# An attention and MoE chain: row maxima on ScalarE's DMA queue, later inversion of the sums, a reordered prelude and other first banks

## The chip, the core and the metric

The kernel runs on one core of one Trainium2 chip. The metric is device time in microseconds (us), lower is better; a run is compared with other runs on the same chip. Five engines work side by side, each through its own queue in program order: TensorE (PE in the profile), VectorE (DVE), ScalarE (ACT), GpSimd (POOL) and SyncE (SP), which here does nothing but issue DMAs. An engine that meets a wait holds everything behind it in its own queue.

## The reference

Clustered attention (2 batches, 8 heads, 768 tokens, head size 64, 16 centroids per head), and then two MLPs on its output ("MoE" in the code).

```python
q_assign = np.argmax(np.einsum('bhsd,hcd->bhsc', q_n, c_n), axis=-1)   # q_n, k_n, c_n: normalised
k_assign = np.argmax(np.einsum('bhsd,hcd->bhsc', k_n, c_n), axis=-1)
mask = q_assign[:, :, :, None] == k_assign[:, :, None, :]
scores = np.where(mask, scale * np.matmul(q, k.transpose(0, 1, 3, 2)), -1000000000.0)
scores = scores - np.max(scores, axis=-1, keepdims=True)
attn = np.exp(scores)
attn = attn / (np.sum(attn, axis=-1, keepdims=True) + 1e-09)
x = np.matmul(attn, v)                       # reshaped to 1536 tokens x 512
x = np.maximum(x @ w_in, 0.0) ** 2 @ w_out   # first MLP, 512 -> 2048 -> 512
h = x @ w_in2                                # second MLP
return (h * np.cos(h)) @ w_out2
```

## The kernel before

Attention works on 8 pairs `n` of heads (one batch, two heads side by side on the 128 partitions). A pair has two halves `hf` of 384 query rows, and a half is 6 units of one 128-key tile each, so a pair has 12 units and the whole has 96. One loop over steps `g` from -9 to 95 does everything: step `g` computes `scores(g)` (four pairs of matmuls, L410, then the exponential on ScalarE, L414) and, nine units ahead, `s_max(g + 9)` (four matmuls, L359, and VectorE's maximum, L362); `pv` (L433) follows two units at a time in odd steps. PSUM is three double banks `unit`, handed out in turn by `unit()` and `give()`, and two banks `o_ps` for `pv`. An engine's queue has the order of the code; within a step the phases PRE, then scores, s_max and pv, then PROD, then POST are run, and the tables `prep`, `prep_second`, `prep_all` and `finish` say at which step and in which phase each piece stands.

The **row maximum** of a half reaches the scores through rows of the tile that the fourth pair of matmuls reads (`d["lq"]`, tile `set`). `max_parts` (L371, L372) joins the maxima, `max_rows` (L381) turns them on TensorE, and one step later `stage_max` copies them out of PSUM on ScalarE (`mr`, L388) and places them with two DMAs issued by SP (L391). This stands two steps ahead of the half's first scores.

The **sums** of a half: GpSimd adds up the exponentials (`add_up`, L426; VectorE does it for the last pair), `sums` turns them into column sums on TensorE (L448), `move_sums` copies (L456), `invert` takes the reciprocal on VectorE (L471), writes it to DRAM by SP (`row`, L473) and, once that has landed, reads it back spread over partitions with two more DMAs of SP (`rb`, L476). `divide` (L480) multiplies `o_ps` by it, `combine` (L492, L493) splits the result into two parts `xh` and `xl`. The next half that uses the same `o_ps` must wait for `divide`.

`invert` of one half and `stage_max` of a later one stand in neighbouring steps: `invert` in POST of a step `g` with `g % 6 == 3`, `stage_max` in PRE of the step after it. In SP's queue the order there is `row`, `rb`, `rb`, `mr`, `mr`.

Preparing a pair: loads of q and k, transposes (L249), a full copy and a high part on ScalarE (L265, L258), a low part on VectorE (L271), similarities with the centroids (`sims`, L300), their maximum (`by_token`, `at_max`), a one-hot code (`one_hot`), and the DMAs that place these (`stage`, `stage_own`, `stage_oh`). Pair 0 is prepared in the prelude ahead of the loop, pair 1 by `prep_second`. `warm` sends small matmuls whose result is not used.

Weights of the MLPs are split into a high and a low part by six instructions of VectorE and one copy of ScalarE (`w_split`, L152 to L161); one piece at a time is put at the end of steps 1, 4 and 7 of each pair in the middle of the loop (two pieces each), and in every step from step 75 on.

The MoE steps then run matmuls into `h_bank` (L604) and, two steps later, `y_mm` (L657) into four banks `y_banks` (both halves of `unit1` and `unit2`). The first step also does the last two `pv`, and `sums_here` of the last half into `unit2`.

Of the kernel before, what the change touches and what calls it, by code (L numbers as in the profile page):

```python
# [34 lines left out]
def tile_kernel(ctx: ExitStack, tc: tile.TileContext, q, k, v, centroids, w1i, w1o, w2i, w2o, out):  # L35
# [42 lines left out]


    firstf = perm.tile([P, P], F32, name="firstf")  # L80
    nc.gpsimd.memset(firstf, -1.0)
    nc.gpsimd.affine_select(
        firstf, firstf, pattern=[[1, P]], compare_op=ALU.is_gt, fill=0.0, base=0, channel_multiplier=-1
    )
    nc.gpsimd.affine_select(
        firstf.rearrange("p (b c) -> p b c", c=NC), firstf.rearrange("p (b c) -> p b c", c=NC),
        pattern=[[-NC, P // NC], [0, NC]], compare_op=ALU.is_ge, fill=0.0, base=0, channel_multiplier=1,
    )
    nc.gpsimd.tensor_tensor(firstf, firstf, ident, ALU.add)
    first_of = perm.tile([P, P], BF16, name="first_of")  # L90
    nc.vector.tensor_copy(first_of[:, : 2 * GC], firstf[:, : 2 * GC])
    nc.vector.tensor_scalar(first_of[:, 2 * GC :], firstf[:, 2 * GC :], -1.0, None, ALU.mult)
    oh_above = perm.tile([P, 1], F32, name="oh_above")
    nc.gpsimd.memset(oh_above[: 2 * GC], 0.5)
    nc.gpsimd.memset(oh_above[2 * GC :], -0.5)
    oh_scale = perm.tile([P, 1], F32, name="oh_scale")
    nc.gpsimd.memset(oh_scale[: 2 * GC], 1.0)
    nc.gpsimd.memset(oh_scale[2 * GC :], -BIG)
# [285 lines left out]
    def stage_max(n, hf):  # L384
# [5 lines left out]
        for j in range(2):  # L390
            nc.sync.dma_start(  # L391
# [116 lines left out]
    nc.scalar.activation(eps, half_t, AF.Exp)  # L508
    nc.gpsimd.memset(eps, 1e-9)
    nc.gpsimd.memset(cb, 0.0)  # L510

    def constants(e, i):
        inner = slice(R, P - R)
# [9 lines left out]
    constants(nc.vector, 0)  # L523
    warm(WARM)
    transpose_in(0, "q")
    transpose_in(0, "k")
    full_copy(0, "q")
    full_copy(0, "k")
    load_raw(1, "qk")
    nc.vector.tensor_tensor(c2, cw, cw, ALU.mult)  # L530
# [413 lines left out]
```

## Time and profile before

| what | us |
|---|---|
| runs (three) | 840.76, 838.58, 840.36 |
| median | 840.36 |
| the profiled execution | 838.24 |
| its span, first to last instruction | 836.5 |
| TensorE busy | 794.2 (95%) |
| VectorE busy | 592.6 (71%) |
| ScalarE busy | 357.2 (43%) |
| GpSimd busy | 177.3 (21%) |

The prelude takes the first 35 us or so, the attention loop lasts until about 292 us, and the MoE steps fill the rest. A busy TensorE is not one at its peak, and it is busy with warming matmuls too. The span is 1.7 us shorter than the execution's own time. What follows is read from the waits by engine, the timeline and the windows (busy time and granted clock of a stretch).

### The profile page before, as it was taken

The page shows a single profiled execution, that of the slowest core. Times are in us where ns is not written, and L with a number is a line of the kernel's source. Part 1 is how long each engine was busy: PE and PEld are TensorE (multiplying, and loading weights), DVE is VectorE, ACT ScalarE, POOL GpSimd, SP SyncE. Part 2 cuts the span into 40 slices and gives each one's busy share as a digit, 9 for nine tenths or more (in the row PEclk, how much of TensorE's full clock was granted, in tenths as well). Part 3 has the DMA queues.
Part 4 walks back from the last instruction along what each step waited for, and adds up shares of the span by engine and source line. Part 5 has one row for each costly group of instructions (what it writes and reads, how often), then busy time and mean ns, then how long its engine had stood idle before and what let it go on. Part 6 is the DMA issues. An engine that isn't in the chain of part 4 may idle for free.

```text
span 836.5 us, 11709 instructions
## 1 busy us (share of the span) xinstructions
PE 794.2 (95%) x4453; PEld 591.7 (71%) x4453; DVE 592.6 (71%) x944; ACT 357.2 (43%) x591; POOL 177.3 (21%) x203
## 2 busy tenths in 40 slices
PE   6999999899989799999999999999999999999997
PEld 4655555565555468888888888887788888888886
DVE  5766677676666899795977421969999866666665
ACT  2355454464444444444444342544343433333332
POOL 5254466456545033000000000001222100000000
PEclk9999999999999899999999999999999999999999
DMA  4525244333252390103740000653000100010001
GB/s 110 131 63 136 64 120 98 88 88 82 62 158 67 118 348 1 52 1 123 229 146 5 1 1 26 209 168 101 0 1 1 51 1 1 1 39 13 1 0 51
DMA packets 72376, 61.79 MB, mean 74 GB/s; under 512 B 41288, under 2 KB 63616, under 8 KB 72320
## 3 DMA queue, kind: packets, MB, share of 16 engines
q1 hardware_dynamic: 70768, 60.65, 24.7%
q8 instruction: 35, 0.57, 0.3%
q10 hardware_dynamic: 1552, 0.39, 0.2%
q14 instruction: 21, 0.17, 0.1%
HBM read 47.87 MB, written 5.29 MB: 64 GB/s over the span
## 4 chain that ended last, share of the span: by engine, by line
PE 77%; DVE 7%; DMA 6%; SPq 3%; ACT 2%; issue 2%; DVEq 0%; ACTq 0%
PE unit L657 29%; PE unit L604 16%; PE o_ps L604 14%; PE unit L410 7%; PE o_ps L433 5%; DMA set<-mr 4%; PE unit L359 3%; DMA row<-r 2%; DVE r L471 2%; SPq L476 1%; PE unit L448 1%; DVE ews L626 1%; PE unit L249 1%; DVE ews L625 1%; SPq L345 1%
## 5 line engine op out<-in xcount | busy, mean ns | idle before, releaser
L657 PE MATMUL unit<-w,ewr 128*128 128x512 f32 x576 | 140.2, 392 | 1.9 <-ACT ewr L638 0.7
L657 PE MATMUL unit<-ewr,w 128*128 128x512 f32 x576 | 141.9, 394 | 0.0
L362 DVE TENSOR_REDUCE m<-unit 128x2 f32<-128x768 f32 x96 | 91.4, 952 | 64.1 <-PE unit L359 63.6
L604 PE MATMUL unit<-xh,w 128*128 128x512 f32 x400 | 132.5, 392 | 3.4 <-ACT ews L619 1.9
L657 PEld LDWEIGHTS unit<-w,ewr 128*128 128x128 f32 x576 | 107.9, 188 | 26.8 <-ACT ewr L638 1.1
L657 PEld LDWEIGHTS unit<-ewr,w 128*128 128x128 f32 x576 | 107.9, 187 | 25.7
L604 PE MATMUL o_ps<-xh,w 128*128 128x512 f32 x368 | 121.2, 390 | 0.0
L414 ACT ACTIVATE p<-unit 128x768 f32<-128x768 f32 x96 | 77.7, 812 | 99.6 <-PE unit L410 97.7
L410 PE MATMUL unit<-set,set 64*128 64x384 f32 x512 | 87.4, 377 | 19.7 <-DMA set<-mr 17.3
L642 POOL TENSOR_TENSOR ewr<-ews,ewr 128x512 fp32r<-128x512 f32 x24 | 33.3, 1388 | 329.3 <-ACT ewr L638 297.6
L604 PEld LDWEIGHTS unit<-xh,w 128*128 128x128 f32 x400 | 75.1, 188 | 22.3 <-ACT ews L619 3.0
L642 DVE TENSOR_TENSOR ewr<-ews,ewr 128x512 fp32r<-128x512 f32 x72 | 49.5, 688 | 53.6 <-ACT ewr L621 51.4
L426 POOL TENSOR_TENSOR acc<-acc,p 128x384 f32<-128x384 f32 x84 | 86.7, 1067 | 3.2 <-ACT p L414 3.2
L410 PEld LDWEIGHTS unit<-set,set 64*128 64x128 f32 x512 | 48.0, 187 | 53.6 <-DMA set<-mr 22.5
L604 PEld LDWEIGHTS o_ps<-xh,w 128*128 128x128 f32 x368 | 69.1, 188 | 15.2
L629 ACT ACTIVATE ews<-ews,hpi 128x512 f32<-128x512 f32 x48 | 34.8, 725 | 103.0 <-DVE ews L628 103.0
L604 PE MATMUL unit<-xl,w 128*128 128x512 f32 x200 | 78.3, 391 | 0.0
L433 PE MATMUL o_ps<-p,rawv 128*64 128x384 f32 x384 | 74.6, 510 | 0.0
L604 PE MATMUL o_ps<-xl,w 128*128 128x512 f32 x184 | 71.9, 391 | 0.0
L153 DVE SCALAR_TENSOR_TENSOR w<-aux,aux 128x512 fp32r<-128x512 f32 x64 | 49.2, 768 | 1.8
L158 DVE SCALAR_TENSOR_TENSOR aux<-wraw,aux 128x512 f32<-128x512 uint32 x64 | 46.3, 723 | 1.8
L433 PEld LDWEIGHTS o_ps<-p,rawv 128*64 128x64 f32 x384 | 23.8, 139 | 30.6 <-issue 30.5
(128 smaller groups left out, 1080.8 us busy)
## 6 DMA issues: line engine op xcount, KB each, us to landing
wraw<-in_moe_w_in_dram SPq DMA_DIRECT2D x32, 512.0 KB, 4.2
wraw<-in_moe_w_out_dram SPq DMA_DIRECT2D x32, 512.0 KB, 3.9
rawq<-in_q_dram SPq DMA_DIRECT2D x8, 384.0 KB, 4.3
ext<-set SPq DMA_DIRECT2D x32, 96.0 KB, 2.1
rawv<-in_v_dram SPq DMA_DIRECT2D x8, 384.0 KB, 4.0
out_dram<-outs SPq DMA_DIRECT2D x12, 256.0 KB, 2.7
rawk<-in_k_dram SPq DMA_DIRECT2D x7, 384.0 KB, 5.0
rb<-row SPq DMA_DIRECT2D x28, 96.0 KB, 2.7
```

The costliest lines, as they stand in the source:

```text
L153: ve.scalar_tensor_tensor(w[:, 1], restf, 2.0**-20, power.bitcast(F32), ALU.mult, ALU.mult)
L158: cost(690, lambda: ve.scalar_tensor_tensor(restf, low, 2.0**-32, rest, ALU.mult, ALU.add)),
L359: nc.tensor.matmul(u[:, j, :HALF], lhsT=a[r, qs], rhs=b[r, ks], start=(p == 0), stop=(p == 1))
L362: nc.vector.tensor_reduce(d["m"][:, i, :, kh], u[:, :, :HALF], AX, ALU.max)
L410: nc.tensor.matmul(u[:, j, :HALF], lhsT=a[r], rhs=b[r, qs], start=(p == 0), stop=(p == len(ops) - 1))
L414: nc.scalar.activation(t, u[:, :, :HALF], AF.Exp, scale=SCALE)
L426: e.tensor_tensor(accs[hb][:, j], a[:, j], ptiles[u_][:, j], ALU.add)
L433: nc.tensor.matmul(o_ps[hf][j * D : (j + 1) * D, :HALF], lhsT=raw[n, "v"][:, kt, j, :], rhs=t[:, j], start=(kt == 0), stop=(kt == NT - 1),)
L604: nc.tensor.matmul(ph, lhsT=w[:, a, :], rhs=x[blk][:, a, :], start=(a == i == 0), stop=(a == KD - 1 and i == 2))
L629: nc.scalar.activation(e2, e2, AF.Sin, bias=hpi)
L642: e.tensor_tensor(al, e2, ah.bitcast(F32), ALU.subtract)
L657: nc.tensor.matmul(y, lhsT=a, rhs=b, start=(idx in opens and i == 0), stop=(idx in closes and i == 2))
```

## The change

Seven things change.

1. The two DMAs of `stage_max` are issued by ScalarE and no longer by SP. Of pair 0's one-hot DMAs the two for k are ScalarE's too.
2. `invert`, `divide` and `combine` stand one step later (10 and 15 for 9 and 14).
3. `max_rows` runs in a new phase LAST, behind the other PROD pieces of its step.
4. In the prelude the centroids are loaded first, and their chain (norm, reciprocal, transpose, `cb`) stands ahead of the transposes of q and k; constants move from VectorE to GpSimd, the making of `first_of` and its kin goes behind the first of these and its two copies to ScalarE.
5. The 24 warming matmuls between `sims(0)` and `one_hot(0)` go, and pair 1's transposes move in among them.
6. Pair 1's similarity steps move into steps -4 to -1, its stages to other steps.
7. The first MoE step's h goes to `banks[0]`, the second's to `y_banks[3]`, and from the third on the four banks rotate; `sums_here` of the last half uses `unit1`.

```diff
-    def stage_oh(n):
+    def stage_oh(n, e=nc.sync):
...
-                nc.sync.dma_start(
+                (e if i else nc.sync).dma_start(
...
         for j in range(2):
-            nc.sync.dma_start(
+            nc.scalar.dma_start(
                 d["lq"][OUTER[j], hf * HALF : (hf + 1) * HALF].bitcast(F32), mr[j * R : (j + 1) * R].bitcast(F32)
             )
...
+    nc.sync.dma_start(cw, centroids.rearrange("h c d -> (h c) d"))
     load_raw(0, "q")
     load_raw(0, "k", nc.scalar)
-    nc.sync.dma_start(cw, centroids.rearrange("h c d -> (h c) d"))
...
     stage(0, "k")
     stage_own(0)
+    sims(0)
+    by_token(0)
     low_part(0, "q")
     stage(0, "q")
-    low_part(0, "k")
-    sims(0)
-    warm(WARM_STEP)
-    by_token(0)
-    warm(WARM_STEP)
+    transpose_in(1, "q")
     at_max(0)
-    warm(WARM_STEP)
-    one_hot(0)
-    stage_oh(0)
-    transpose_in(1, "q")
     full_copy(1, "q")
     high_part(1, "q")
+    one_hot(0)
+    stage_oh(0, nc.scalar)
+    low_part(0, "k")
...
     load_raw(0, "v")
-    sims(1)
...
-    def h_bank(idx):
-        return banks[idx % (2 if idx < 4 else 4)]
...
-        ph = h_bank(idx)
+        ph = banks[(idx - 2) % 4] if idx > 1 else (banks[0], y_banks[3])[idx]
...
     prep_second = [
-        (-12, PROD, by_token),
-        (-12, POST, stage_own),
-        (-10, PROD, at_max),
-        (-8, PROD, one_hot),
-        (-11, POST, stage, "k"),
-        (-11, POST, stage, "q"),
-        (-7, PRE, stage_oh),
+        (-10, POST, stage_own),
+        (-8, POST, stage, "k"),
+        (-7, POST, stage, "q"),
+        (-7, PROD, sims),
+        (-6, PROD, by_token),
+        (-5, PROD, at_max),
+        (-4, PROD, one_hot),
+        (-4, POST, stage_oh),
         (1, PRE, load_raw, "v"),
     ]
     prep_all = [
         (6, PRE, max_parts, 0),
-        (6, PROD, max_rows, 0),
+        (6, LAST, max_rows, 0),
         (7, PRE, stage_max, 0),
         (12, PRE, max_parts, 1),
-        (12, PROD, max_rows, 1),
+        (12, LAST, max_rows, 1),
         (13, PRE, stage_max, 1),
     ]
 
     finish = [
         (8, PROD, sums),
         (9, PRE, move_sums),
-        (9, POST, invert),
-        (14, PRE, divide),
-        (14, POST, combine),
+        (10, POST, invert),
+        (15, PRE, divide),
+        (15, POST, combine),
     ]
...
         run(g, PROD)
+        run(g, LAST)
         run(g, POST)
...
-        0: [lambda: pv(NU - 2), lambda: pv(NU - 1), lambda: sums_here(last + 1, units[2])],
+        0: [lambda: pv(NU - 2), lambda: pv(NU - 1), lambda: sums_here(last + 1, units[1])],
```

ScalarE's queue ahead of a first half (pair 2, steps 9 to 11): `p` are the exponentials, `mxb` is `by_token`'s copy, `xh` `combine`'s, `mr` the row maxima. Before:

```order
L414 ACTIVATE p_1041<-unit_66 128x768
L318 COPY mxb_1060<-mx_1058 128x384
L388 CAST mr_1073<-unit_67 64x384
L414 ACTIVATE p_1085<-unit_65 128x768
L414 ACTIVATE p_1107<-unit_65 128x768
```

Now, in ScalarE's queue at the same place:

```order
L393 ACTIVATE p_1013<-unit_66 128x768
L297 COPY mxb_1029<-mx_1027 128x384
L471 CAST xh_87<-x_1001 128x128
L471 CAST xh_88<-x_1001 128x256
L367 CAST mr_1043<-unit_66 64x384
L370 DMA set_2_112<-mr_1043 32x384 x2
L393 ACTIVATE p_1055<-unit_67 128x768
L393 ACTIVATE p_1083<-unit_67 128x768
```

Two copies and two DMAs have come between `mxb` and the next exponential. In both listings the last two exponentials read the same unit, so the later one's scores wait for the earlier one's exponential.

VectorE's queue ahead of a second half (pair 2, steps 3 to 6): `r` is the reciprocal of the sums, `m` the maxima of `s_max`, `aux` and `w` are pieces of a weight split, the last row is the low part of q. Before:

```order
L471 RECIPROCAL r_1206<-r_1206 128x192
L362 TENSOR_REDUCE m_1222<-unit_67 128x2
L161 TENSOR_SCALAR aux_309<-top_312 128x512
L153 SCALAR_TENSOR_TENSOR w_1_0_1271<-aux_310,aux_309 128x512
L362 TENSOR_REDUCE m_1222<-unit_67 128x2
L271 TENSOR_TENSOR set_2_122<-unit_65,set_0_120 128x768
```

Now, in VectorE's queue at the same place:

```order
L341 TENSOR_REDUCE m_1196<-unit_66 128x2 x2
L450 RECIPROCAL r_1180<-r_1180 128x192
L140 TENSOR_SCALAR aux_279<-top_282 128x512
L132 SCALAR_TENSOR_TENSOR w_1_0_1247<-aux_280,aux_279 128x512
L341 TENSOR_REDUCE m_1196<-unit_66 128x2
L250 TENSOR_TENSOR set_2_108<-unit_67,set_0_106 128x768
```

The reciprocal has moved behind the maximum of the next step, right ahead of the two split pieces, the next maximum and the low part.

SP's queue around pair 1's first half, before:

```order
L473 DMA row_713<-r_678 4x192
L476 DMA rb_715<-row_713 64x384 x2
L391 DMA set_2_122<-mr_720 32x384 x2
L290 DMA ext_1_129<-set_1_125 32x768 x2
L290 DMA ext_0_128<-set_2_126 32x768 x2
```

Now, in SP's queue there:

```order
L452 DMA row_715<-r_654 4x192
L455 DMA rb_717<-row_715 64x384 x2
L269 DMA ext_1_115<-set_1_111 32x768 x2
L269 DMA ext_0_114<-set_2_112 32x768 x2
```

The pair of `mr` DMAs is gone from behind `row` and `rb`; the rest keeps its order.

## Rows read from the trace of the kernel before

**Rows 1.** Windows: start:end, us, busy us (instructions) by engine, clock, DMA, GB/s.

```profile
34.00:237.00 203.00, 190.28 (x1592) 115.70 (x1592) 138.83 (x176) 103.66 (x171) 108.72 (x114) 1.00 0.38 93
237.00:292.00 55.00, 44.59 (x337) 26.02 (x335) 39.81 (x63) 22.61 (x38) 20.63 (x20) 0.91 0.36 115
```

**Rows 2.** Waits of PE (us, times, longest): 50 to 237, 245 to 292, MoE start.

```profile
PE unit L410 <- DMA set<-mr: 7.6, 9, 1.4
...
PE unit L410 <- DMA set<-mr: 9.6, 3, 4.9
...
PE unit L604 <- ACT ews L619: 1.9, 2, 1.2
```

**Rows 3.** Timeline ahead of a first half: start, us, engine, line, [idle before <-releaser].

```profile
124.41 1.35 DVE L471 RECIPROCAL r<-r 128x192 f32<-128x192 f32 x1
...
124.94 0.47 ACT L388 CAST mr<-unit 64x384 fp32r<-64x384 f32 x1
125.31 0.80 ACT L414 ACTIVATE p<-unit 128x768 f32<-128x768 f32 x1
...
125.78 0.55 SPq L473 DMA_DIRECT2D row<-r  x1
126.17 0.62 PE L410 MATMUL unit<-set,set 64*128 64x384 f32 x4 [0.16 <-ACT p L414]
...
128.64 1.21 SPq L391 DMA_DIRECT2D set<-mr  x2
...
130.88 0.78 PE L410 MATMUL unit<-set,set 64*128 64x384 f32 x2 [0.94 <-DMA set<-mr]
```

**Rows 4.** Timeline of ScalarE's start: the one DMA that it issues itself.

```profile
0.81 0.71 ACTq L224 DMA_DIRECT2D rawk<-in_k_dram  x1
...
1.55 1.28 ACT L508 ACT_TABLE_LOAD   x1 [1.55 <-PEq L929]
```

**Rows 5.** Timeline ahead of a second half (pair 4).

```profile
173.86 0.81 ACT L414 ACTIVATE p<-unit 128x768 f32<-128x768 f32 x1 [0.47 <-PE unit L410]
...
175.01 1.26 DVE L161 TENSOR_SCALAR aux<-top 128x512 uint32<-128x512 uint32 x1
...
176.31 1.38 DVE L153 SCALAR_TENSOR_TENSOR w<-aux,aux 128x512 fp32r<-128x512 f32 x1
...
177.60 0.95 DVE L362 TENSOR_REDUCE m<-unit 128x2 f32<-128x768 f32 x1
...
178.47 0.94 DVE L271 TENSOR_TENSOR set<-unit,set 128x768 fp32r<-128x768 f32 x1
...
179.59 0.87 PE L249 MATMUL unit<-ident,rawk 128*128 128x128 f32 x6
```

**Rows 6.** Timeline of the last pairs, 246 to 289 us.

```profile
246.20 0.61 PE L410 MATMUL unit<-set,set 64*128 64x384 f32 x2 [3.44 <-DMA set<-mr]
...
280.21 1.49 PE L410 MATMUL unit<-set,set 64*128 64x384 f32 x6 [4.93 <-DMA set<-mr]
...
281.00 0.55 DVE L480 TENSOR_TENSOR x<-o_ps,rb 128x384 f32<-128x384 f32 x1
...
283.35 1.03 DVE L426 TENSOR_TENSOR acc<-p,p 128x384 f32<-128x384 f32 x2 [1.80 <-ACT p L414]
...
288.15 1.51 PE L433 MATMUL o_ps<-p,rawv 128*64 128x384 f32 x8
```

**Rows 7.** Windows right behind the two longest waits: columns as in rows 1.

```profile
246.20:251.15 4.95, 4.95 (x26) 2.96 (x27) 3.31 (x5) 1.62 (x2) 0.00 (x0) 0.66 0.89 263
...
280.20:284.98 4.78, 4.77 (x20) 2.46 (x20) 2.91 (x7) 2.09 (x3) 0.00 (x0) 0.53 0.76 303
```

**Rows 8.** Timeline: a split piece while GpSimd has no additions.

```profile
279.21 0.69 DVE L153 SCALAR_TENSOR_TENSOR w<-aux,aux 128x512 fp32r<-128x512 f32 x1
```

**Rows 9.** Timeline: pair 2's load of q, its transposes; below, all such loads' median.

```profile
34.08 0.68 SPq L224 DMA_DIRECT2D rawq<-in_q_dram  x1
...
42.26 0.88 PE L249 MATMUL unit<-ident,rawq 128*128 128x128 f32 x6
...
rawq<-in_q_dram SPq DMA_DIRECT2D x8, 384.0 KB, 4.3
```

More of the change, by code (lines that the diff above doesn't have):

```diff
@@ L76, in tile_kernel @@
     nc.gpsimd.memset(eps, 1e-9)
[L80 to L98, printed above, removed]
     hpi = perm.tile([P, 1], F32, name="hpi")
@@ L521, in constants_own, with selection @@
                 e.memset(t[rows, S:].bitcast(F32), -1.0 / R)
[L523 to L536 removed]
+    def selection():
+        firstf = perm.tile([P, P], F32, name="firstf")
+        nc.gpsimd.memset(firstf, -1.0)
+        nc.gpsimd.affine_select(
+            firstf, firstf, pattern=[[1, P]], compare_op=ALU.is_gt, fill=0.0, base=0, channel_multiplier=-1
+        )
+        nc.gpsimd.affine_select(
+            firstf.rearrange("p (b c) -> p b c", c=NC), firstf.rearrange("p (b c) -> p b c", c=NC),
+            pattern=[[-NC, P // NC], [0, NC]], compare_op=ALU.is_ge, fill=0.0, base=0, channel_multiplier=1,
+        )
+        nc.gpsimd.tensor_tensor(firstf, firstf, ident, ALU.add)
+        first_of = perm.tile([P, P], BF16, name="first_of")
+        nc.scalar.copy(first_of[:, : 2 * GC], firstf[:, : 2 * GC])
+        nc.scalar.activation(first_of[:, 2 * GC :], firstf[:, 2 * GC :], AF.Copy, scale=-1.0)
+        oh_above = perm.tile([P, 1], F32, name="oh_above")
+        nc.gpsimd.memset(oh_above[: 2 * GC], 0.5)
+        nc.gpsimd.memset(oh_above[2 * GC :], -0.5)
+        oh_scale = perm.tile([P, 1], F32, name="oh_scale")
+        nc.gpsimd.memset(oh_scale[: 2 * GC], 1.0)
+        nc.gpsimd.memset(oh_scale[2 * GC :], -BIG)
+        return first_of, oh_above, oh_scale
+    warm(WARM)
     nc.vector.tensor_scalar(cn, cn, 1e-6, None, ALU.add)
@@ L550, in tile_kernel @@
         )
+    transpose_in(0, "q")
+    transpose_in(0, "k")
+    full_copy(0, "q")
+    full_copy(0, "k")
+    load_raw(1, "qk")
+    constants(nc.gpsimd, 0)
+    first_of, oh_above, oh_scale = selection()
+    constants_own(nc.gpsimd, 0)
+    constants(nc.gpsimd, 1)
+    for i in range(1, 3):
+        constants_own(nc.gpsimd, i)
+    high_part(0, "q", nc.vector)
+    high_part(0, "k", nc.vector)
     stage(0, "k")
     stage_own(0)
+    sims(0)
+    by_token(0)
     low_part(0, "q")
     stage(0, "q")
-    low_part(0, "k")
-    sims(0)
-    warm(WARM_STEP)
-    by_token(0)
-    warm(WARM_STEP)
+    transpose_in(1, "q")
     at_max(0)
-    warm(WARM_STEP)
-    one_hot(0)
-    stage_oh(0)
-    transpose_in(1, "q")
     full_copy(1, "q")
     high_part(1, "q")
+    one_hot(0)
+    stage_oh(0, nc.scalar)
+    low_part(0, "k")
     low_part(1, "q")
@@ L796, in moe @@
         assert not pending and not splitting
-    PRE, PROD, POST = range(3)
+    PRE, PROD, LAST, POST = range(4)
     prep = [
```

13 lines of the change are left out of this document (4 added, 9 removed).

## The prediction

> **What bounds the kernel now.** Read first the windows: from 34 to 237 us TensorE is busy 190.28 of 203.00 us, from 237 to 292 us only 44.59 of 55.00, and there the granted clock's mean is 0.91 [rows 1]. So the attention loop is bound by TensorE, and what can be won in it is TensorE's idle time, most of it late. Then the waits of TensorE: `scores` (L410) waits for the placed row maxima 7.6 us in nine places up to 237 us, and 9.6 us in three places behind [rows 2]. Then the timeline of one place, to see why these DMAs are late. The copy `mr` starts at 124.94 and takes 0.47, so the data is there at 125.41, but SP issues the DMA at 128.64: ahead of it in SP's queue stand `row`, issued at 125.78 when the reciprocal (124.41, 1.35 long) is done, and `rb`, which waits until `row` has landed. The scores that read the maxima stand still 0.94 and go on at 130.88 [rows 3]. Twice it is far worse: 3.44 and 4.93 us [rows 6]. Behind these two the granted clock is 0.66 and 0.53 on average of 4.95 and 4.78 us in which TensorE is busy throughout [rows 7]: part of both stretches ran at 1.2 instead of 2.4 GHz, after TensorE had done nothing for 3.44 and 4.93 us.
>
> **The change, part by part.** All terms are against the profiled execution's 838.24 us; minus is a gain.
>
> *Waits removed in the middle.* With ScalarE issuing right behind its own copy, the maxima land some 3 us earlier, and no wait for them remains: -7.6 up to 237 us [rows 2]. This is the cover that I cost at nothing: landing in time needs only that ScalarE is not late itself.
>
> *What ScalarE pays.* The two DMAs now stand in ScalarE's queue, and behind them the exponential of the same step. The only DMA that ScalarE issues before the change takes 0.71, and the next instruction of its queue, a table load that needs no data, starts at 1.55, when it is over (0.81 + 0.71) [rows 4]. So an issue blocks the queue. The price of two: SP's same pair takes 1.21 [rows 3]; the bounds are nothing (issue and exponential overlap) and 1.42 (two of 0.71). I take 1.21, the row of the same DMAs. Before, the exponential started at 125.31, 0.10 before the copy ended; now it must start 1.21 and about 0.1 of handover behind its end: 1.4 later. Who waits for that: the next step's scores use the same unit and started at 126.17, right behind that exponential (125.31 + 0.80) and after a wait for it [rows 3]. So all of 1.4 is on the path, in the six first halves of pairs 1 to 6: +8.4. The copies of `combine` now also stand ahead of `mr`, while `by_token` runs earlier; both are about as long as one copy, and I let them cancel. In second halves the exponential has 0.47 to spare, waiting for scores [rows 5]; the rest, 0.9, is hidden there by the next item, which is longer.
>
> *What the later reciprocal does to second halves.* It moves from a step in which VectorE waits for TensorE into the next, between that step's maximum and two split pieces. Before, these run back to back: 175.01 + 1.26, 176.31 + 1.38, then the maximum at 177.60, then the low part of q, 178.47 + 0.94 = 179.41, and right behind it TensorE's transposes of k at 179.59, which need the unit that the low part frees [rows 5]. Pushed by 1.35 [rows 3], the low part ends at 180.76 and the transposes start at about 180.85: 1.25 later. This holds where a split piece stands in that step and a later pair is transposed, in pairs 1 to 5: five times, +6.2. Bounds: 0, if VectorE finds idle time that I overlook, and 2.7, twice the reciprocal (below). In first halves it goes behind the comparison of `at_max`, where nothing in TensorE's queue waits for it.
>
> By the Trainium skill (SBUF — State Buffer, "Who interferes with whom"), a VectorE instruction with two inputs in SBUF contends with a GpSimd instruction that reads SBUF. The trace agrees: the second split piece takes 1.38 there [rows 5] and 0.69 where GpSimd adds nothing [rows 8]. If the pieces moved past GpSimd's additions, each of the five would cost 0.69 less, 2.8 in all instead of 6.2, and the forecast would be 3.4 lower; GpSimd is busy 108.72 of 203.00 us [rows 1], so I don't count on it.
>
> *The late waits.* First, at 246.20: 3.44 is gone, and so is the stretch at the lower clock. With a mean clock of 0.66, the busy 4.95 us would have taken 0.66 of that, 3.27, at the higher one: 1.7 more. The later exponential costs 0.9 here. -3.44 - 1.7 + 0.9 = -4.2. Second: 9.6 - 3.44 - 4.93 = 1.2, less 0.9: -0.3. Third, at 280.21: 4.93, and 4.78 x (1 - 0.53) = 2.2 for the clock, 7.1 in all. But VectorE is behind by then: it was busy through this wait, reached `divide` at 281.00 and only then stood still for 1.80 [rows 6]. `divide` now stands one step later, behind an addition (1.03) and two more split pieces (0.69 at most each [rows 8]): 281.00 + 1.03 + 1.38 + 0.55 = 283.96. The `pv` that overwrites its bank ran at 288.15 [rows 6], so it can come 4.2 earlier and no more: -4.2.
>
> *MoE's first banks.* Both waits of L604 for ScalarE's first function, 1.9 [rows 2], come from a bank of the same tile being read; the new banks are in other tiles: -1.9. Bounds 0 and -1.9.
>
> *The prelude.* Without the 24 warming matmuls and with VectorE's work regrouped, pair 0's scores can start earlier. What is late next is pair 2's q: its load was issued at 34.08 and used at 42.26, 8.18 later [rows 9]. It stands in SP's queue behind pair 1's four one-hot DMAs, which are now made three steps later, while two `mr` DMAs ahead of it are gone. Net two more, 1.2 by SP's pair [rows 3]: if the load has no slack, +1.2. If it lands in the median 4.3, it is there at 34.08 + 1.2 + 4.3 = 39.6: up to -2.7. With weights and k in flight the slow end is nearer; I take 0.
>
> *Sum:* -7.6 + 8.4 + 6.2 - 4.2 - 0.3 - 4.2 - 1.9 + 0 = -3.6. 834.6 for an execution like the profiled one; the median is 2.1 above that one (840.36 against 838.24), so 836.8.
>
> **The rivals.**
>
> *Cheap issue.* ScalarE's issue overlaps its exponential, or takes far less than SP's. Then 8.4 and twice 0.9 fall away: -13.8, 826.6. For it: nothing in the trace shows the issue of so small a DMA by ScalarE. Against it: rows 4. The Trainium skill (DMA: Bandwidth & Descriptors, "Issuing engines are not separate DMA queues") says that issuing on several engines only saves the sequencer's time of initiating, usually small beside the DMA. By it this rival would be right on ScalarE's side, 826.6. Rows 3 show what the rule leaves out, an issue held up by the queue's order.
>
> *VectorE becomes the bound of second halves; slower than before.* The low part of q is late, so are the transposes of k, and if VectorE has no idle time left over steps 4 to 8, k's low part, too, waits for the reciprocal: 2 x 1.35 = 2.7 in each of five pairs, 13.5 instead of 6.2. -3.6 + 7.3 = +3.7: 844.1. It turns the sign from 2.0 per pair on (6.2 + 3.6 = 9.8 by five). For it: no gap between the four VectorE instructions of rows 5. Against: VectorE is busy 138.83 of 203.00 [rows 1].
>
> *The last wait gives nothing.* The last reciprocal, too, is a step later, behind more of VectorE's own work, and its way through DRAM shares the DMA engines with weight loads. If `rb` lands 4.2 later than VectorE would come to `divide`, `pv` runs at 288.15 as before: -3.6 + 4.2 = +0.6, 841.0.
>
> **How the numbers follow.** Forecast 0.42, cheap issue 0.25, VectorE bound 0.20, last wait 0.13. A measurement of this kernel can tell about 0.3%, 2.5 us, from no change. Around the forecast, the prelude's ends (-2.7, +1.2) and the contention (-3.4) let it fall between -9.7 and -2.4, and the second halves' doubt puts a third of it above -2.5. Faster: 0.25 + 0.42 x 0.62 = 0.51. Slower: most of the second rival, a little of the others, 0.21. Within: 0.28. The range goes from just below the first rival, 825.5, to just above the second, 844.5; a first rival without the second halves' cost (-20.0, 820.4) stays out.
>
> **What would show it.** Right: no wait of L410 for `set<-mr`; in its place waits of L410 for the exponential in first halves, and the exponential about 1.3 behind `mr`'s end; transposes of k in second halves right behind a low part that ends over 1 us later; clock 1.00 at 246 and 280; `pv` waiting for L480 near the loop's end; no wait of L604. Wrong, if DMAs of ScalarE take little, if the reciprocal finds a gap, or if `set<-mr` still waits, since ScalarE's copy is itself late.

## The result and the profile after

The changed kernel takes 845.02 us (median of 20 runs, 840.56 to 848.04) against 840.28 us for the kernel before on the same chip: a ratio of 1.0058 with an interval of 1.0043 to 1.0073. It is slower by 0.6%, where 836.8 us, faster by 0.4%, was forecast; the time lies just above the range's upper end of 844.5. The profiled execution took 840.91 us with a span of 839.2, so it is one of the shorter ones; why the median lies 4 us above it is asked in the last part but one of the experiments. One of the 20 runs of the kernel before took 1104.15 us and is left out of the ratio.

The totals of busy time hardly move (TensorE 794.2 to 789.0, VectorE 592.6 to 595.7, ScalarE 357.2 to 358.4). What moved is seen when the same events are looked up in both timelines (start of the first exponential of a pair, start of a group of 12 `h_mm` matmuls; us):

| event | before | after | difference | made in the stretch ahead | forecast |
|---|---|---|---|---|---|
| first exponential, pair 0 | 35.26 | 34.74 | -0.5 | -0.5 | 0 |
| first exponential, pair 6 | 230.12 | 238.06 | +7.9 | +8.5 | +7.0 |
| first group of `h_mm` | 292.64 | 289.88 | -2.8 | -10.7 | -8.7 |
| 5th group | 314.41 | 314.95 | +0.5 | +3.3 | -1.9 |
| 51st group | 569.58 | 567.80 | -1.8 | -2.3 | 0 |
| end of the last matmul | 832.15 | 834.81 | +2.7 | +4.4 | 0 |

So in the profiled execution the attention loop came out near the forecast in sum, and the whole sign was lost behind it, in the MoE steps, which I had costed at 1.9 us of gain and then not looked at again.

The windows of the kernel after, columns as in [rows 1], show the trade in the loop: TensorE is busy less in the middle and more late, and the late clock is back at 1.00.

```profile
34.00:237.00 203.00, 179.25 (x1514) 110.99 (x1513) 139.06 (x167) 100.08 (x163) 108.12 (x110) 0.99 0.38 89
237.00:292.00 55.00, 50.95 (x423) 31.13 (x423) 45.53 (x74) 27.21 (x45) 23.90 (x24) 1.00 0.48 147
```

Waits of TensorE after, 50 to 237 us (total, times, longest), to be held against the first row of [rows 2]: not one wait for `set<-mr` is left, and these five stand there. Three of them were there before, but shorter: `scores` for the exponential 0.9, the transposes for `mr`'s unit 1.8, `scores` for the maxima 0.4.

```profile
PE unit L389 <- ACT p L393: 11.8, 10, 1.6
PE unit L306 <- ACT mr L367: 3.7, 6, 0.7
PE unit L389 <- DVE m L341: 2.4, 6, 0.5
PE unit L338 <- DMA ext<-ot: 1.5, 3, 0.5
PE unit L228 <- DVE set L250: 1.0, 4, 0.2
```

The timeline after, ahead of pair 4's first half, answers [rows 3]: the copy ends at 163.24, the two DMAs hold ScalarE's queue for 1.16, the exponential starts 1.29 behind the copy, and the scores that need its unit stand still for 1.55.

```profile
162.77 0.47 ACT L367 CAST mr<-unit 64x384 fp32r<-64x384 f32 x1
163.27 1.16 ACTq L370 DMA_DIRECT2D set<-mr  x2
...
164.53 0.81 ACT L393 ACTIVATE p<-unit 128x768 f32<-128x768 f32 x1 [1.29 <-PE unit L306]
165.40 0.62 PE L389 MATMUL unit<-set,set 64*128 64x384 f32 x4 [1.55 <-ACT p L393]
```

The timeline after, ahead of pair 4's second half, answers [rows 5]: the later reciprocal, two split pieces, the maximum and the low part of q follow one another on VectorE as the order said, but TensorE's transposes wait only 0.25 for them. TensorE was itself late by then, by a wait of 0.61 for ScalarE's exponential in the step of the reciprocal.

```profile
180.52 1.34 DVE L450 RECIPROCAL r<-r 128x192 f32<-128x192 f32 x1
...
181.02 0.62 PE L389 MATMUL unit<-set,set 64*128 64x384 f32 x4 [0.61 <-ACT p L393]
...
182.34 1.38 DVE L132 SCALAR_TENSOR_TENSOR w<-aux,aux 128x512 fp32r<-128x512 f32 x1
...
184.51 0.94 DVE L250 TENSOR_TENSOR set<-unit,set 128x768 fp32r<-128x768 f32 x1
...
185.51 0.87 PE L228 MATMUL unit<-ident,rawk 128*128 128x128 f32 x6 [0.25 <-DVE set L250]
```

The start of the MoE steps, timeline after, and behind it the window of the matmuls that follow. The 4th group of `h_mm` (its start is the last row of the timeline) writes `banks[1]`, the second half of the tile whose first half holds the 3rd group. ScalarE reads that one at L616, but ahead of L616 in its queue stands `combine`'s copy (L471), which waits for `divide` (L459), which waits for the last reciprocal. TensorE stands still for 3.75 and then runs at a clock of 0.60 on average. The tile that the 3rd and 4th groups share isn't new: the kernel before has the same two halves there (`idx % 2` for the first four groups). What is new is that the 1st and 2nd, and the 2nd and 3rd, no longer share it, so that TensorE comes to the 4th group without having waited.

```profile
303.43 2.54 DVE L446 RECIPROCAL rb<-rb 128x384 f32<-128x384 f32 x1
306.11 0.56 DVE L459 TENSOR_TENSOR x<-o_ps,rb 128x384 f32<-128x384 f32 x1
...
306.70 0.51 ACT L471 CAST xh<-x 128x384 fp32r<-128x384 f32 x1 [5.27 <-DVE x L459]
...
307.12 0.59 ACT L616 ACTIVATE ews<-unit 128x512 f32<-128x512 f32 x1
...
307.76 0.65 PE L601 MATMUL unit<-xh,w 128*128 128x512 f32 x1 [3.75 <-ACT ews L616]
```

```profile
307.70:312.00 4.30, 4.24 (x12) 3.32 (x13) 4.16 (x6) 1.78 (x4) 2.52 (x2) 0.60 0.60 214
```

The same happens once more where the second MLP begins, in a place that the forecast never came to. With the new rotation groups 51 and 52 of `h_mm` have the two halves of one tile; with the old one these two had `o_ps`, two tiles. Group 52 must wait until VectorE has read group 51 (L622), and VectorE is late there because it has just added up and split the first MLP's output. Timeline and window after:

```profile
577.10 0.68 DVE L622 SCALAR_TENSOR_TENSOR ews<-ews,unit 128x512 f32<-128x512 f32 x1
...
577.83 0.80 PE L601 MATMUL unit<-xh,w 128*128 128x512 f32 x1 [4.40 <-DVE ews L622]
```

```profile
577.80:582.00 4.20, 4.17 (x12) 3.32 (x13) 3.01 (x5) 0.72 (x1) 0.51 (x1) 0.62 0.00 0
```

### The profile page after: what moved, and what is told of

Read it like the earlier page. It is cut to its first block, busy times and chain, and to the rows that moved or that the text cites. A ratio compares the mean times of both kernels' runs of the same rounds, so it can differ in the third digit from the quotient of the medians.

```text
span 839.2 us, 11598 instructions
## 1 busy us (share of the span) xinstructions
PE 789.0 (94%) x4429; PEld 592.5 (71%) x4429; DVE 595.7 (71%) x938; ACT 358.4 (43%) x593; POOL 182.4 (22%) x207
## 4 chain that ended last, share of the span: by engine, by line
PE 75%; DVE 13%; DMA 4%; ACT 3%; issue 2%; SPq 2%; ACTq 1%; DVEq 0%
PE unit L654 29%; PE unit L601 15%; PE o_ps L601 14%; PE unit L389 5%; PE o_ps L412 4%; PE unit L338 3%; DVE m L341 2%; DMA rawq<-in_q_dram 2%; DVE aux L137 2%; PE unit L228 1%; ACTq L370 1%; DVE set L250 1%; ACT p L393 1%; SPq L324 1%; DVE acc L405 1%
## 5 line engine op out<-in xcount | busy, mean ns | idle before, releaser
L601 PE MATMUL unit<-xh,w 128*128 128x512 f32 x400 | 134.8, 399 | 8.4 <-DVE ews L622 4.6
L654 PE MATMUL unit<-ewr,w 128*128 128x512 f32 x576 | 139.8, 391 | 0.0
L389 PE MATMUL unit<-set,set 64*128 64x384 f32 x512 | 79.7, 368 | 14.5 <-ACT p L393 11.8
L389 PEld LDWEIGHTS unit<-set,set 64*128 64x128 f32 x512 | 42.1, 185 | 41.7 <-ACT p L393 25.7
L137 DVE SCALAR_TENSOR_TENSOR aux<-wraw,aux 128x512 f32<-128x512 uint32 x64 | 49.3, 771 | 1.8
L139 DVE SCALAR_TENSOR_TENSOR top<-wraw,top 128x512 uint32<-128x512 uint32 x64 | 49.4, 772 | 1.7
```

The source lines that it names most:

```text
L137: cost(690, lambda: ve.scalar_tensor_tensor(restf, low, 2.0**-32, rest, ALU.mult, ALU.add)),
L139: cost(690, lambda: ve.scalar_tensor_tensor(top, high, 0xC0000000, top, ALU.bitwise_and, ALU.bitwise_or)),
L389: nc.tensor.matmul(u[:, j, :HALF], lhsT=a[r], rhs=b[r, qs], start=(p == 0), stop=(p == len(ops) - 1))
L601: nc.tensor.matmul(ph, lhsT=w[:, a, :], rhs=x[blk][:, a, :], start=(a == i == 0), stop=(a == KD - 1 and i == 2))
L654: nc.tensor.matmul(y, lhsT=a, rhs=b, start=(idx in opens and i == 0), stop=(idx in closes and i == 2))
```

## The experiments

### The MoE banks: alone, and taken out of the changed kernel

My first theory after the result: the new banks cost some 4 us at the second MLP's start and nothing is won by them elsewhere. The rival is my own term, -1.9. `b_new_banks` is the kernel before with

```diff
-        ph = h_bank(idx)
+        ph = banks[(idx - 2) % 4] if idx > 1 else (banks[0], y_banks[3])[idx]
...
-        0: [..., lambda: sums_here(last + 1, units[2])],
+        0: [..., lambda: sums_here(last + 1, units[1])],
```

The expectations count the groups from 0: their h 50 and h 51 are groups 51 and 52 of this text.

> The kernel before, with the new MoE banks and the sums of the last half in unit1, nothing else. My prediction's term: -1.9, 838.4. Theory from the traces: in the rotation h 50 and 51 now share a tile, and they stand right behind the long VectorE work at the end of the first MLP, so TensorE waits 4.4 there and then runs at the lower clock: +4.5 at that place, -2.3 in the steps before it, -1 to +2 at the start: 841 to 844.

Measured: 843.83 us, before 840.07; ratio 1.0048 (1.0033 to 1.0062). Alone they cost 3.8 us. The two waits of [rows 2] at the MoE start are indeed gone, 1.17 ahead of group 2 and 0.69 ahead of group 3. But one ahead of group 4 has come, so from the 1st group to the 5th only 0.5 is won (21.25 for 21.77):

```profile
PE unit L604 <- ACT ews L619: 1.4, 1, 1.4
```

and the timeline has the wait at group 52:

```profile
578.59 0.79 PE L604 MATMUL unit<-xh,w 128*128 128x512 f32 x1 [4.32 <-DVE ews L625]
```

The gain of 2.3 in the first MLP, which this expectation put down to the banks, did not appear: groups 5 to 51 take 255.17 here as in the kernel before. It belongs to the prelude (below).

`a_old_banks` is the changed kernel with these two edits undone.

> The changed kernel, with the banks of the MoE steps and of the last half's sums as before. If the new banks cost in the changed kernel what they cost alone (3.75): 841.3, with no wait at h 51 and 0.2 more per step in the first MLP. By my prediction's term (-1.9 for the change): 846.9.

Measured: 835.78 us, before 839.50; ratio 0.9964 (0.9950 to 0.9978). By medians that is 9.2 less than the changed kernel, by the two ratios 7.9; the profiled spans differ by 7.5 (831.7 against 839.2). So the banks cost twice as much in the changed kernel as alone. Its waits at the MoE start and at the second MLP's start show why: three small waits for ScalarE in place of one of 3.7, and 1.6 in place of 4.4 (the kernel before has 1.5 there), and the granted clock stays at 1.00 behind both. From the 1st group to the 5th it takes 22.47, the changed kernel 25.07, and from the 51st to the end 263.08 against 267.00. A part of the first difference is the last reciprocal: counted from the 1st group, it starts 1.0 later in the changed kernel, behind a split piece (L137) of 1.67 that takes 0.69 here.

```profile
PE unit L604 <- ACT ews L619: 2.4, 3, 1.2
```

```profile
PE unit L604 <- DVE ews L625: 1.6, 1, 1.6
```

Without the banks, then, the change is faster than the kernel before, and 1 us from the forecast of 836.8. But the forecast contained 1.9 of gain from them; without that it was 838.7.

`a_first_ahead` leaves the banks and changes ScalarE's order in the third MoE step, so that L616 no longer stands behind the last reciprocal.

```diff
                 if steps[idx][0] == 0 and idx < FA:
                     ew_last(idx, nc.gpsimd)
+            if idx == 2:
+                invert_here(last + 1), divide(last + 1), combine(last + 1)
...
-        2: [lambda: invert_here(last + 1), lambda: divide(last + 1), lambda: combine(last + 1)],
```

> The changed kernel, with the inversion, division and combination of the last half moved behind the reading of h 2 in the third MoE step: ScalarE no longer stands behind the last reciprocal before it frees the tile that h 3 needs. Theory 1 (the late gain is given back there by ScalarE's order): TensorE's wait of 3.75 for ews goes and so does the lower clock behind it (1.7): 5.4 less, about 839.5. Theory 2 (VectorE, busy 11.6 of the 12 us from 292 to 304, is the bound whatever the order): the wait comes back one or two matmul groups later, for o_ps or for a weight piece, and the time stays within 2 us of 845.

Measured: 839.93 us, before 840.07; ratio 1.0007 (0.9987 to 1.0027): 5.1 less than the changed kernel by medians, 4.3 by ratios. Its profiled execution is the longest of its ten (845.24), and its loop ends 8.2 later than the changed kernel's in the profile, so only what follows can be compared: from the 1st group to the 5th 19.40 for 25.07. From 290 to 325 us the view lists one wait of TensorE alone. It is one of `pv`, still in the loop, which the changed kernel has too; none is left in the first MoE steps:

```profile
PE o_ps L412 <- DVE x L459: 0.9, 1, 0.9
```

So the 3.75 were ScalarE's order and not a lack of VectorE's time, although VectorE is busy 11.59 of the 12 us from 292 to 304 in the changed kernel.

### The loop: each cure alone, and each taken out

The change holds two cures for one illness, the maxima that come late out of SP's queue: they go to another queue, and `row` and `rb` go a step later, behind them. Theory 1 was that ScalarE's issue is the expensive part, theory 2 that VectorE's later reciprocal is. Four kernels tell them apart. `a_sp_issue` is the changed kernel with

```diff
-            nc.scalar.dma_start(
+            nc.sync.dma_start(
                 d["lq"][OUTER[j], ...
```

and `b_act_issue` is the kernel before with the opposite. `b_invert_late` is the kernel before with

```diff
-        (9, POST, invert),
-        (14, PRE, divide),
-        (14, POST, combine),
+        (10, POST, invert),
+        (15, PRE, divide),
+        (15, POST, combine),
```

and `a_invert_back` is the changed kernel with the opposite.

> The changed kernel, with the two DMAs of stage_max issued by SP again; invert stays one step later, so in SP's queue the mr DMAs now stand ahead of row and rb. Theory 1 (ScalarE's issue is what costs: 1.16 us per pair of DMAs, 1.56 us of TensorE's wait for the exponential in each of six first halves, 0.61 in second halves, 0.7 instead of 0.3 for mr's unit): no wait of scores for set<-mr and none above 0.3 for the exponential; 6 x 1.56 + 3 x 0.61 + 6 x 0.4 = 13.6 us less, about 831 to 835. Theory 2 (the later reciprocal on VectorE costs, 1.25 in each of five second halves): the waits stay in other clothes and the time is at most 4 us lower, 841 or more. Theory 3 (SP's queue is still late): set<-mr waits come back, 7 us or more.

> The changed kernel, with invert, divide and combine at their old steps (9, 14); the mr DMAs stay with ScalarE. Theory 1 (ScalarE's issue costs, the reciprocal's place little): the 1.56 us waits for the exponential stay, TensorE's waits of 0.44 for VectorE's maximum go, 842 to 845. Theory 2 (the reciprocal's place costs 1.25 in five second halves): about 6 us less, 839. Both: no long set<-mr wait at the end, since ScalarE issues.

> The kernel before, with the two DMAs of stage_max issued by ScalarE and nothing else. Theory 1: the waits for set<-mr go (7.6 in the middle, 9.6 late, with the clock 3.9), six waits of 1.5 and some of 0.6 for the exponential come (9 to 13), and of the late gain most is lost again at the start of the MoE steps, where TensorE waits for VectorE's last reciprocal: 836 to 842. Cheap issue: 825 or less.

> The kernel before, with invert, divide and combine one step later and nothing else: in SP's queue the mr DMAs come ahead of row and rb. Theory 1: set<-mr waits go, ScalarE pays nothing, TensorE loses at most 0.6 per half to VectorE; 7.6 in the middle is kept, the late gain is partly lost at the MoE start: 829 to 834. Theory 2 (the later reciprocal costs 1.25 in five second halves): 836 to 839.

| kernel | us | ratio to before (840.29) | interval |
|---|---|---|---|
| `a_sp_issue` | 840.82 | 1.0016 | 0.9997 to 1.0035 |
| `a_invert_back` | 837.93 | 0.9972 | 0.9957 to 0.9986 |
| `b_act_issue` | 836.75 | 0.9950 | 0.9928 to 0.9973 |
| `b_invert_late` | 834.23 | 0.9926 | 0.9905 to 0.9946 |

Each cure alone gains (ScalarE's issue 3.5, the later reciprocal 6.1), and taking either out of the changed kernel gains too (ScalarE's issue 4.2, the later reciprocal 7.1). Neither theory had that: taken out, the cures came near the numbers of theory 2, alone near those of theory 1. Two cures for one illness are paid twice and cure once. How much the second costs hangs on the banks: with the old ones (`a_old_banks`) both cures, edit 3 and the new prelude gain 3.7 together, and the prelude alone gains 1.8 of that (below), so both cures together still gain less than either alone. The waits of `b_invert_late`, 50 to 237 us, show a price that neither theory had named: TensorE's `s_max` waits for a DMA, though not for that of the maxima.

```profile
PE unit L359 <- DMA ext<-ot: 5.0, 4, 2.1
PE unit L327 <- ACT mr L388: 4.2, 6, 0.8
PE unit L410 <- DVE m L362: 2.6, 6, 0.4
PE unit L359 <- DVE m L362: 2.0, 3, 1.1
```

Its timeline around 200 us shows whose queue it is: SP issues `row`, then stands still until `row` has landed (199.81 to 200.89), issues `rb`, and only then what stands next in line, a later pair's copies into `ext` (L290) and behind them its one-hot codes (L345, `ext<-ot`), for which TensorE stands still.

```profile
199.27 0.54 SPq L473 DMA_DIRECT2D row<-r  x1
...
200.89 1.13 SPq L476 DMA_DIRECT2D rb<-row  x2
202.12 3.14 SPq L290 DMA_DIRECT2D ext<-set  x4
...
205.37 2.44 SPq L345 DMA_DIRECT2D ext<-ot  x4
...
208.68 0.54 PE L359 MATMUL unit<-ext,ext 64*128 64x384 f32 x2 [1.09 <-DMA ext<-ot]
```

### The illness itself: SP standing still behind `row`

If SP's wait for `row` is the cause, then nothing else has to change its engine or its step; `rb` alone has to be issued after something else. In the kernel before SP waits 15.3 us for `row`, in 14 places, 1.8 at most. `b_rb_split` is the kernel before with

```diff
         nc.sync.dma_start(row.rearrange("j (h c) -> (j h) c", h=2), r[0:P:R])
+        rbs[hb] = row
+
+    def spread(hb):
+        row = rbs[hb]
         rb = rbs[hb] = ap.tile([P, HALF], F32, tag="rb", name=f"rb{hb}", bufs=2)
         for j in range(2):
...
         (9, POST, invert),
+        (10, POST, spread),
```

> The kernel before, with nothing changed but rb's two DMAs: SP issues them one step after row, so behind the mr DMAs of that step; the reciprocal, divide and combine stay where they were. Theory 1 (what costs is SP standing still behind row until it has landed, and everything that stands behind rb waits with it: mr before, the one-hot ext DMAs when invert is a step later): no wait of scores for set<-mr, none of s_max for ext, none for ScalarE's exponential above 0.3; 7.6 in the middle and about 10 late are gained, and the start of the MoE steps gives part of the late gain back: 824 to 831. Theory 2 (the maxima are late for another reason, or rb one step later makes divide late): waits for set<-mr or of pv for divide's x remain, 836 or more.

Measured: 818.59 us, before 840.07; ratio 0.9747 (0.9731 to 0.9763). It is 21.5 us faster than the kernel before and 26.4 faster than the changed one, below its own expectation. SP's queue in the timeline now reads `row`, `mr`, `rb`, without a gap:

```profile
121.92 0.55 SPq L473 DMA_DIRECT2D row<-r  x1
...
122.57 1.23 SPq L391 DMA_DIRECT2D set<-mr  x2
...
123.88 0.55 SPq L480 DMA_DIRECT2D rb<-row  x1
```

and of the waits from 50 to 225 us the 7.6 of [rows 2] are gone, with nothing new in their place but 1.0 more for the loads of q and 1.0 for a low part:

```profile
PE unit L327 <- ACT mr L388: 1.8, 6, 0.3
PE unit L249 <- DMA rawq<-in_q_dram: 1.6, 2, 1.4
PE unit L249 <- DVE set L271: 1.0, 4, 0.2
PE unit L410 <- ACT p L414: 0.9, 6, 0.2
```

Behind 225 us the cure is not whole: of the late waits for the maxima two are left, against the expectation, and behind the longer one (261.17) the clock falls to 1.2 GHz once more:

```profile
PE unit L410 <- DMA set<-mr: 3.0, 2, 2.7
```

On this kernel, where in the middle of the loop SP is no longer late, the two cures can be priced without the illness. `c_act` issues the `mr` DMAs from ScalarE (the edit of `b_act_issue`).

> The kernel with rb issued a step after row (818.59), with the mr DMAs issued by ScalarE: there SP is never late, so this is the price of ScalarE's issue alone. My prediction's term, 1.4 in each of six first halves: +8.4, 827. From the traces so far: 1.56 in first halves, 0.6 in second ones, and about 1 of lower clock behind each long one: +13 to +17, 832 to 836. If ScalarE's issue cost nothing: 818 to 819.

Measured: 837.36 us, before 839.25; ratio 0.9977 (0.9959 to 0.9995). ScalarE's issue alone costs 18.8 us, more than any theory had, and the kernel is then as slow as `b_act_issue`, whose SP is late: with ScalarE issuing, SP's order decides nothing any more. Its waits from 50 to 237 us, and a window behind one of them:

```profile
PE unit L410 <- ACT p L414: 12.8, 11, 1.9
```

```profile
132.00:136.00 4.00, 3.49 (x18) 2.08 (x20) 0.96 (x1) 1.26 (x2) 2.17 (x3) 0.64 0.38 111
```

A pair (1 to 4, from first exponential to first exponential) takes 33.85 on average against 31.19 in `b_rb_split`, 2.7 more. TensorE's idle time is 1.3 of that (2.53 against 1.24 per pair); most of the other half is the clock, which stands at 1.2 GHz for a stretch behind such a wait.

`c_late` was to price the later reciprocal: `b_rb_split` with all four steps of `finish` one later (10, 11, 15, 15).

> The kernel with rb issued a step after row, with reciprocal, rb, divide and combine all one step later: SP stands still for nothing, so this is the price of VectorE's and ScalarE's new order alone. My prediction's term, 1.25 in each of five second halves: +6.2, 825. If all of it was SP's order in disguise: 818 to 820. From the waits seen with the late inversion (for VectorE's maxima, for mr's unit, for the low part; 7 in all, and some lower clock): 824 to 829.

Measured: 839.77 us, ratio 1.0001 (0.9983 to 1.0020). It priced something else. `rb` now comes behind the one-hot DMAs of the same step, lands late, and TensorE's `pv` stands in the same step as `divide` and waits for it; so the rise of 21 says nothing on the reciprocal alone.

```profile
PE o_ps L433 <- DVE x L484: 10.8, 5, 2.5
```

`c_more_vector` moves nothing and instead adds, at the place where the changed kernel has its reciprocal, a second one of the same size on a tile that nobody reads:

```diff
         (10, POST, spread),
+        (10, POST, extra),
...
+    def extra(hb):
+        nc.vector.reciprocal(ones_r, ones_r)
```

> The kernel with rb issued a step after row (818.59), with a second reciprocal of the same size on a tile that nobody reads, in VectorE's queue where the changed kernel has its reciprocal; nothing else moves. My prediction's term (1.25 in each of five second halves, by the low part of q): 824 to 825. From the waits seen with the late inversion (0.25 for the low part, 0.4 for a maximum in each half): 820 to 824, by many small waits for VectorE. If VectorE finds idle time for it: 818.6.

Measured: 823.94 us, before 839.50; ratio 0.9821 (0.9805 to 0.9836): 5.4 above `b_rb_split` by medians, 6.2 by the two ratios. The waits from 50 to 228 us, to be held against those of `b_rb_split`, show 2.8 of it as waits of `s_max` for VectorE's maxima, while the wait for the low part stays at 1.0; the rest shows in no wait of this view:

```profile
PE unit L361 <- DVE m L364: 2.8, 4, 0.9
...
PE unit L251 <- DVE set L273: 1.0, 4, 0.2
```

### The prelude

`b_prelude` is the kernel before with the edits 4, 5 and 6 of the change and the half of edit 1 that concerns pair 0's one-hot DMAs.

> The kernel before, with the new prelude and pair 1's regrouped preparation and nothing else. My prediction's term: 0, between -2.7 and +1.2. Theory from the traces: pair 0 starts about 0.5 to 1 earlier, then waits 1.7 for pair 2's q, whose load is issued later: +0 to +2, 840 to 842. Rival (the prelude's chain was late itself): 837.5.

Measured: 838.23 us, before 840.07; ratio 0.9978 (0.9964 to 0.9992), a gain of 1.8, though not where it was meant. The loop starts 0.8 earlier, and pair 1 then starts 2.9 later, since pair 0 waits 1.9 in one place for pair 2's q. The loop ends 2.1 later in the profiled execution (first group of `h_mm` 294.70 for 292.64). What pays is the first MLP, groups 5 to 51 in 252.85 for 255.17, so that the two profiled executions are equal (838.32 and 838.24) and the 1.8 stands in the medians: from 320 to 440 us TensorE is busy throughout at a clock of 1.00 in both kernels, yet it gets through 531 matmuls here and 521 in the kernel before (windows of before, then of `b_prelude`).

```profile
320.00:440.00 120.00, 120.00 (x521) 97.35 (x520) 98.22 (x173) 54.30 (x92) 5.75 (x4) 1.00 0.29 97
```

```profile
320.00:440.00 120.00, 120.00 (x531) 99.38 (x530) 100.57 (x176) 56.69 (x96) 5.39 (x4) 1.00 0.29 97
```

In `b_prelude` neighbouring matmuls of this window start 226 or 227 ns apart, every one; in the kernel before 224 to 240, 231 on average, most of it in `y_mm` (232.9 for 226.6). All kernels here with the new prelude have the 252.85 and none without it. What of it does so isn't known and wasn't tried.

### The changed kernel once more

> The changed kernel as it is, for one more profiled execution. Theory (the 1.56 us waits for the exponential are each long enough to put TensorE at 1.2 GHz behind them in many executions, so that the time moves with how many do): several stretches of granted clock well under 1.00 between 34 and 237 us, each right behind such a wait, and more of them the longer the execution takes than 840.9. Rival (the median lies above the profiled execution for another reason, say the loads of the prelude): the clock in the loop is as in the first profile, one stretch.

Measured: 846.40 us, with a span of 844.6. The waits for the exponential are about the same (10.2 us in 9 places for 11.8 in 10), but the clock behind them isn't. One wait of 1.55, ahead of pair 4's first half, ends at 165.40 in the first profile of the changed kernel and at 166.99 in this one. In the four microseconds from 168 on, behind both, TensorE starts 35 matmuls in the first and 17 in the second:

```profile
168.00:172.00 4.00, 4.00 (x35) 2.56 (x33) 2.57 (x4) 1.62 (x2) 2.23 (x3) 1.00 0.51 137
```

```profile
168.00:172.00 4.00, 4.00 (x17) 1.57 (x15) 0.96 (x1) 0.81 (x1) 3.09 (x4) 0.50 0.24 74
```

This execution has four such stretches between 40 and 210 us, three behind waits of 1.55 and one behind a wait of 1.70 for pair 2's q; the first profile has one. From the first `h_mm` group on, the two executions take the same time to 0.1 us. So the loop, and in it the clock, makes the 4 us between the first profile and the median, as far as two executions can show it.

### A better kernel

`c_best` joins what gained: the new prelude, `b_rb_split`'s order with SP issuing, the order of `a_first_ahead`, and a rotation in which the halves of one tile alternate with `o_ps`; edit 3 is in it too. `c_best2` differs in the phase of that rotation.

```diff
-        if idx < 4:
-            ph = (banks[0], y_banks[3], banks[0], banks[1])[idx]
+        if idx < 5:
+            ph = (banks[0], y_banks[3], banks[0], banks[1], banks[3])[idx]
         else:
-            ph = (banks[2], banks[0], banks[3], banks[1])[idx % 4]
+            ph = (banks[0], banks[2], banks[1], banks[3])[idx % 4]
```

> The changed kernel's prelude and first two banks, with the mr DMAs on SP, inversion at its old step and rb a step after row, ScalarE freed of the last reciprocal in the third MoE step, and from h 4 on a rotation in which banks of one tile alternate with o_ps. Against 818.59: prelude -1.8, no wait at the MoE start -2, no same-tile wait in the first MLP -2 to -3, and no 4.4 at its end: 811 to 815. If the prelude's late load of pair 2's q holds the faster loop back, or VectorE bounds the MoE start: 816 to 819.

> c_best (816.74), with the rotation's phase shifted: h 48 and 50 in the two halves of one tile, h 49 and 51 in o_ps. If the tile shared with h 49 is what h 51 waits for: that wait of about 3 and the lower clock behind it go, 812 to 814. If VectorE's work at the end of the first MLP holds TensorE whatever the bank: 816 to 817.

Measured: 816.74 us (ratio 0.9739, 0.9720 to 0.9757) and 815.09 us (ratio 0.9711, 0.9696 to 0.9725). Group 52's wait for VectorE, 2.9 in `c_best`, is this in `c_best2`:

```profile
PE unit L608 <- DVE ews L641: 0.6, 1, 0.6
```

So the tile that groups 50 and 52 shared in `c_best` was what group 52 waited for. `c_best2` beats both kernels, by 2.9% and 3.5%. `c_best` came out in the second case of its expectation and `c_best2` 1 us above its first: TensorE still waits for the loads of q, 3.2 us in two places up to 236 us (1.6 in `b_rb_split`).

## Why the prediction was wrong

The step that failed is "MoE's first banks ... -1.9. Bounds 0 and -1.9". It took the change of banks for two waits that vanish, and bounded a loss out without a reason. Its reading "the new banks are in other tiles" holds for the 2nd group alone, and two things were missed.

First, the 3rd and 4th groups have the two halves of one tile in both kernels. TensorE, no longer held ahead of groups 2 and 3, is held ahead of group 4, by ScalarE behind the last reciprocal: alone by 1.4, so that 0.5 of the 1.9 is won; in the changed kernel by 3.75 with the lower clock behind it, 2.6 more over the first five groups than with the old banks. Second, "from the third on the four banks rotate", by `(idx - 2) % 4` instead of `idx % 4`, moves groups 51 and 52 from `o_ps` into one tile, which VectorE is late to read at the second MLP's start: 4.4 for 1.6. Measured, the banks cost 3.8 alone and 7.9 to 9.2 in the changed kernel. With that the sign turned.

Of the 6.3 between the forecast's 834.6 for a profiled execution and 840.91, the MoE steps but for groups 5 to 51 make +9.6 (+7.7 where -1.9 was forecast); groups 5 to 51 make -2.3 and the loop with the prelude -1.1. The other 2 of the error lie in the median, which is 4.1 above the profiled execution where 2.1 was taken.

Point by point:

- **What bounds the kernel** was right, and worth more than the forecast made of it. The waits for `set<-mr` and the clock behind two of them add up to 7.6 + 3.44 + 1.7 + 1.2 + 7.1 = 21.0 in the forecast's own terms; `b_rb_split`, which moves `rb` and nothing else, gains 21.5 (19.5 between the two profiled executions). That the two are so near is partly luck: 3.0 of these waits remain there, and the loop up to pair 6 gains 10.7, more than its 7.6 of waits.
- **What ScalarE pays** was right as a mechanism and half too small. The exponential starts 1.29 behind the copy (about 1.3 was named) and the scores wait 1.55 (1.4). But second halves pay too, 0.6 each in four of them where the forecast let 0.9 be hidden; and the clock falls behind waits of 1.5, which I had looked for only behind those of 3 and more. 8.4 and twice 0.9, 10.2, were forecast; `c_act` measures 18.8. In the changed kernel, beside these, `mr`'s unit comes free 0.4 later in first halves, where `combine`'s copies ahead were let cancel against the earlier `by_token`. The rival of the cheap issue is out: two DMAs hold ScalarE's queue for 1.16 us. The Trainium skill (DMA: Bandwidth & Descriptors, "Issuing engines are not separate DMA queues") calls the time of initiating usually small beside the DMA itself; the trace has 0.58 per DMA against 1.9 (median) from issue to landing, and here the exponential stands behind it.
- **The later reciprocal** was right in size, 6.2 against 5.4 to 6.2 (of a stand-in, `c_more_vector`, which adds a reciprocal and moves none), but not in place, so the size agrees by luck: the low part makes the transposes wait 0.25 and not 1.25, and what else is seen are `s_max` and `scores` waiting for maxima. The rival that VectorE becomes the bound of second halves named 844.1, near the measured time, but by 2.7 per pair that no run shows; that it comes near is chance.
- **The middle of the loop**, +7.0 forecast and +8.5 in the profiled execution, therefore agrees by errors of both signs, among them waits for `ext` that the forecast did not have, though its listing of SP's queue showed `ext` standing right behind `rb`.
- **The late waits** went as forecast, -10.7 for -8.7, and `pv` waits for `divide` near the end as named. A part was given back at the MoE start: the loop came 2.8 earlier, the last reciprocal only 0.5 (303.43 for 303.90), and with the new banks TensorE met it in one wait. The last rival had a mechanism of this kind (VectorE's last work caps what the loop gains), but for `pv`, and without the banks.
- **The prelude**, 0 between -2.7 and +1.2, measured -1.8, by the first MLP's matmuls and not by its own stretch. What was named as late next was late: pair 2's q is issued at 37.44 in `b_prelude` for 34.08 before, 3.4 later and not the 1.2 of two more DMAs, and its transposes wait 1.85 for it at 43.31.
- **The range** stopped at the second rival and had no room for a loss in a term that was held to be a sure gain.

The parts, each by its own run, add up to -21.5 + 18.8 + 5.4 + 3.8 - 1.8 = +4.7, and +4.7 was measured. I would not lean on that: `a_old_banks` shows that the banks cost more than 3.8 in the changed kernel and the loop's edits less than this sum, and edit 3 (`max_rows` in LAST) was never run by itself.

## What to carry to other kernels

When a queue that works in program order is late, find the instruction that makes it stand still and move only that one behind the others; moving the victims to another engine makes that engine pay, and moving the whole step moves the wait to the next in line. Price every edit over its whole range of effect: a rotation that changes for the first two steps' sake changes in all of them, and where two neighbours share a tile, look at who reads it late. Two changes that cure the same wait must be priced together, since the second pays in full and gains nothing.

## What was not expected of the hardware

- A wait of TensorE of 1.55 us may or may not be followed by a stretch at 1.2 GHz: at 168 to 172 us, behind the same wait, the granted clock is 1.00 in one execution of the changed kernel and 0.50 in another. The runs of this kernel spread from 840.56 to 848.04 (20 runs), those of `b_rb_split`, which has no such wait there, from 817.99 to 819.06 (4 runs); that the one makes the other is argued and not shown.
- TensorE busy throughout, at a granted clock of 1.00, ran the same matmuls at 521 and at 531 in 120 us in two kernels that differ only far ahead of them. The cause stays open.
